# Another row order for the modulation weights, and a small read of them ahead of the conditioning vector

## The chip, the cores and the metric

The kernel runs on one core of a Trainium2 chip. The metric is the device time of one execution in microseconds (us), the median of several runs. A core has five engines with a queue of instructions each: TensorE (PE in the profile; its weight loads are PEld), VectorE (DVE), ScalarE (ACT), GpSimd (POOL) and SyncE (SP), which here only issues transfers. ScalarE issues transfers too. All transfers are carried out by the core's 16 DMA engines.

## What is computed

One transformer block whose two layer norms are modulated by a conditioning vector c. S is 2048, D is 640, all in bfloat16:

```
mod = (silu(c) @ w_mod).reshape(1, 6, 1, -1)          # w_mod: 640 x 3840
sa, ca, ga, sb, cb, gb = (mod[:, i] for i in range(6))
h = layernorm(x) * (1 + ca) + sa
x = x + ga * attention(h)      # 32 heads of 20, a causal window of 256, wqkv 640 x 1920, wo 640 x 640
h = layernorm(x) * (1 + cb) + sb
x = x + gb * mlp(h)            # (sigmoid(h @ w_gate) * (h @ w_up)) @ w_down, hidden size 1536
```

## The kernel before

The 2048 rows of x are worked on in 8 chunks of 256, each of two blocks of 128 rows. A chunk goes through layer norm 1, the transpose to hT, the projections to Q, K and V, scores and exponentials, the masks (GpSimd), the product with V, the output projection, layer norm 2 and the MLP. The chunks overlap: while one is in attention, the next ones are projected and an earlier one is in its MLP.

**The order of the work** is not found while it runs. `build` lists some 2100 operations, each with the engines it may run on, the places it reads and writes, and its working function. `PRIO` holds one number for each operation: sorted by it, they give the order on every engine, and the remainder by 5 is the engine. `schedule` gives each tile a slot of its pool, `emit` writes out each engine's queue with the semaphore waits that follow from reads, writes and reused slots. Every transfer increments one of 24 semaphores, taken in turn, and waits for the transfer 24 before it.

**The opening**, which the change touches, computes the modulation of layer norm 1 (sa and ca, that is columns 0 to 1279 of w_mod) while the first rows of x are normalised:

- ScalarE issues the transfer of c (`c_row`, 5 partitions of 128 elements), then that of the second block of x, and loads its activation table. SyncE issues the first block of x, then the five pieces of w_mod (`load_bulk`, tag wm0, one for each row group `kt`, 128 rows of 2560 bytes, kept for now in the buffer of wd), then wqkv in four pieces of 320 columns and one of 640 with further blocks of x between them, then the rest of w_mod (wm1, wm2, wm3), wo and the MLP weights. All go through the helper at L570.
- GpSimd writes the identity matrix `ident`. PE runs warm matmuls on a zeroed buffer (L649), two to an operation: three operations, then `ctr` (L634), which turns c into a column of 5 elements on each partition, then a matmul that opens the accumulators of modA, then two more warm operations.
- `ctr` is followed by VectorE's `c_col` (L636), ScalarE's tanh (L637), VectorE's `siluc` (L638) and `silubc` (L640), which spreads silu(c) over 64 columns. In VectorE's order `c_col` stands between the statistics (L776) of the first block of x and those of the second, and `silubc` ahead of those of the second.
- modA: five groups of 10 matmuls with w_mod as the weights and `silubc` as the moving side, one group for each `kt`, with filling matmuls (L660) between them. The transposes of the normalised x (with `ident` as the moving side) stand between the fourth group and the fifth. VectorE copies the result to `mA` (L761).
- The transposed x is copied to `hT` (L839) and modulated there with `mA` (L846 on ScalarE, L847 on VectorE). Then the projections of chunk 0 begin, PE reading `hT` as weights and wqkv as the moving side, and ScalarE and VectorE bring them from PSUM to `stg`, `QT`, `KT` and `V` (L893, L894).
- The first exponentials (L1015) follow on ScalarE. The transfer of the further pieces of w_mod is used later by `mod_rows` for the two gates and the modulation of layer norm 2.

c multiplies w_mod row by row, so a row of w_mod and its element of c must be on the same partition and in the same group `kt`:

```
dma(lambda: c_row, lambda: c.rearrange("o (t p) -> (o t) p", p=128), ..., eng="act")
wm_src = w_mod.rearrange("(t p) f -> p t f", p=128)
... e.matmul(psc.ap[:, 0:NDT], c_row, ident[0:NDT, 0:NDT], start=True, stop=True)
```

With these, row 128t+p is on partition p in group t.

Of the kernel before, what the change touches and what calls it, by code (L numbers as in the profile page):

```python
# [17 lines left out]
NDT = D // 128  # L18
# [7 lines left out]
SWITCH = 0.095  # L26
ENGATTR = {"pe": "tensor", "act": "scalar", "dve": "vector", "pool": "gpsimd", "sp": "sync"}
ENGS = ("pe", "act", "dve", "pool", "sp")
OVERLAP = {"pe": 0.0, "act": 0.085, "dve": 0.075, "pool": 0.045, "sp": 0.0}
# [52 lines left out]
class Prog:  # L82
# [69 lines left out]
    def schedule(self):  # L152


        free = {e: START for e in ENGS}
        bw = 0.0
        lastturn = False
        order = {e: [] for e in ENGS}
        dmacnt = [0] * NDMA
        dmalast = [None] * NDMA  # L160
        rr = 0
        pemode = 0
        portend = 0.0
        freed = {}

        def slot_time(pool, s):
            ten = pool.tenant[s]
            if ten is None:
                if not all(x.done for x in pool.init[s]):
                    return None  # L170
                return max([x.end + x.lat for x in pool.init[s]], default=0.0)
            return None if ten.left else freed[ten]

        def take(t, s):
            ten = t.pool.tenant[s]
            t.prev = list(t.pool.init[s]) if ten is None else list(ten.rel)
            t.slot = s
            t.pool.tenant[s] = t

        for o in sorted(self.ops, key=lambda x: x.prio):  # L180
            assert all(d.done for d in o.deps), o.tag
            e = ENGS[o.prio % 5]
            assert e in o.engs, (o.tag, e)
            o.eng = e
            st = max([o.tmin, free[e] + (SWITCH if e == "pe" and o.mode != pemode else 0.0)]
                     + [d.end + (0.0 if d.eng == "pe" and e == "pe" else d.lat) for d in o.deps])
            if o.isdma and e == "sp":
                st = max(st, bw - QMAX)
            for t in o.tiles:
                if t.slot is None:  # L190
                    step = 1 if t.mate is None else 2
                    best = None
                    for s in range(0, len(t.pool.tenant), step):
                        rts = [slot_time(t.pool, s + k) for k in range(step)]
                        if None not in rts and (best is None or max(rts) < best[0]):
                            best = (max(rts), s)
                    assert best is not None, (o.tag, t.name)
                    if t.mate is None:
                        take(t, best[1])
                    else:  # L200
                        take(t, best[1] + t.odd)
                        take(t.mate, best[1] + 1 - t.odd)
                for x in t.prev:
                    st = max(st, x.end + x.lat)
            if e == "dve" and o.port:
                st = max(st, free["pool"])
            elif e == "pool":
                st = max(st, portend)
            o.start = st
            if e == "pe":  # L210
                pemode = o.mout
            dur = o.dur[e]
            free[e] = st + dur - OVERLAP[e]
            if e == "dve" and o.port:
                portend = free[e]
            if o.isdma:
                turn = o.dlat > 3.0
                if e == "sp" and bw - st > 2.0:
                    free[e] += 0.35 if o.dur[e] > 1.0 else 0.1
                bw = max(st + o.dlat, bw + (MIXED if turn != lastturn and bw > st + o.dlat else 0.0)) + o.work  # L220
                lastturn = turn
                o.end = max(bw - 0.83, st + dur)
                s = rr
                rr = (rr + 1) % NDMA
                dmacnt[s] += 16
                o.key, o.val = f"d{s}", dmacnt[s]
                if dmalast[s] is not None:
                    o.deps.append(dmalast[s])
                dmalast[s] = o
            else:  # L230
                o.end = st + dur
            order[e].append(o)
            o.done = True
            for t in o.tiles:
                t.left -= 1
                if t.left == 0:
                    last = {}
                    for x in t.ops:
                        if x.isdma:
                            last[x] = x  # L240
                    for e2 in ENGS:
                        xs = [x for x in t.ops if x.eng == e2 and not x.isdma]
                        if xs:
                            last[e2] = max(xs, key=lambda x: x.start)
                    t.rel = list(last.values())
                    freed[t] = max(x.end + x.lat for x in t.rel)
        self.order = order
        self.span = max(o.end for o in self.ops)
# [88 lines left out]
def c_pe(n):  # L337
# [3 lines left out]
PE_EPS = 0.14  # L341
PRIO = [
# [124 lines left out]
START = 0.8  # L467
# [839 lines left out]
```

## Time and profile before

| | us |
|---|---|
| median of 3 runs | 325.95 |
| lowest, highest | 325.88, 325.97 |
| span of the profiled execution, first to last instruction | 324.3 |
| median less that span | 1.65 |
| PE busy | 317.3 |
| ACT busy | 212.3 |
| DVE busy | 211.8 |
| POOL busy | 187.2 |

The profile is of one execution. Its span leaves out what lies ahead of the first instruction and behind the last, 1.65 us if it took as long as the median. "Busy" is the time in which an engine has at least one instruction running; the ends of matmuls are modelled. In a timeline row stand the start, the length, the engine, the line of kernel.py, the operation, what is written and read, and in brackets the idle time ahead of it and what ended that. ACTq and SPq are the queues of ScalarE and SyncE while they issue transfers. The share of the DMA engines can pass 1, since several packets can be under way in one engine.

### The profile page before, as it was taken

The numbers are of one execution on the slowest core, as the hardware profiler recorded it, in microseconds if no ns is written. First come the engines' busy times: TensorE is split into PE (matmuls) and PEld (weight loads), VectorE is DVE, ScalarE is ACT, GpSimd is POOL, SyncE is SP. The second block draws the span as 40 slices with busy tenths as digits, with TensorE's granted clock in tenths as the row PEclk, the third lists the DMA queues.
The fourth block names the chain that finished last, engine by engine and source line by source line (L and its number), as shares of the span: only waits on it lengthen the run. The fifth ranks groups of instructions, "written<-read, shape, count | busy, mean of one in ns | idle before, by whom it ended". The sixth has DMA issues, their size and how long they took to land.

```text
span 324.3 us, 11594 instructions
## 1 busy us (share of the span) xinstructions
PE 317.3 (98%) x4872; PEld 222.7 (69%) x4873; DVE 211.8 (65%) x424; ACT 212.3 (65%) x316; POOL 187.2 (58%) x276
## 2 busy tenths in 40 slices
PE   8999999989999999999999999999999999999997
PEld 3564545446776568765776467877786788787885
DVE  5797898778687959674477475837463769264332
ACT  1899985889876687788687867786767764011120
POOL 5128869976668694847585939382939691012100
DMA  7998799989891383824405394340213032202101
GB/s 249 371 333 299 165 269 180 200 137 183 260 164 22 83 109 77 152 61 101 85 22 82 97 103 110 92 69 5 81 40 88 3 79 53 76 20 64 40 2 40
DMA packets 71694, 37.85 MB, mean 117 GB/s; under 512 B 45274, under 2 KB 70362, under 8 KB 71642
## 3 DMA queue, kind: packets, MB, share of 16 engines
q1 hardware_dynamic: 69616, 35.31, 48.3%
q10 hardware_dynamic: 2026, 1.80, 2.1%
q8 instruction: 38, 0.62, 0.8%
q14 instruction: 14, 0.11, 0.1%
HBM read 21.30 MB, written 5.25 MB: 82 GB/s over the span
## 4 chain that ended last, share of the span: by engine, by line
PE 73%; DMA 2%; SPq 2%; DVE 1%; POOL 1%; issue 0%; DVEq 0%
PE M L668 61%; PE S L669 6%; PE M L669 5%; DMA gbc<-gate 2%; SPq L803 2%; DVE wd L1192 1%; POOL x L793 0%; POOL st L788 0%; DVE hh L1211 0%; POOL E L1040 0%; DVE x L1230 0%; DVEq L310 0%
## 5 line engine op out<-in xcount | busy, mean ns | idle before, releaser
L1040 POOL TENSOR_SCALAR_AFFINE_SELECT E<-E 128x512 bf16<-128x512 bf16 (+1 forms) x176 | 142.6, 836 | 68.7 <-ACT E L1015 67.0
L1015 ACT ACTIVATE E<-S 128x512 bf16<-128x512 f32 (+2 forms) x184 | 150.9, 878 | 47.4 <-PE S L669 46.5
L668 PE MATMUL M<-wqkv,hT 128*128 128x480 bf16 (+1 forms) x340 | 73.9, 355 | 0.6 <-ACT hT L846 0.5
L668 PE MATMUL M<-h2T,wu 128*128 128x256 bf16 x480 | 68.0, 273 | 0.5 <-DVE hh L1211 0.5
L668 PE MATMUL M<-h2T,wg 128*128 128x256 bf16 x480 | 67.8, 273 | 0.0
L668 PE MATMUL M<-wd,hh 128*128 128x320 bf16 (+2 forms) x396 | 58.1, 295 | 0.0
L1209 ACT ACTIVATE sig<-M 128x512 f32<-128x512 f32 x48 | 28.9, 602 | 44.1 <-PE M L668 41.7
L1211 DVE SCALAR_TENSOR_TENSOR hh<-sig,M 128x512 bf16<-128x512 f32 x48 | 32.4, 681 | 37.1 <-ACT sig L1209 24.0
L668 PEld LDWEIGHTS M<-h2T,wu 128*128 128x128 bf16 x480 | 45.9, 98 | 8.4 <-issue 1.2
L668 PEld LDWEIGHTS M<-h2T,wg 128*128 128x128 bf16 x480 | 45.7, 98 | 7.1
L668 PEld LDWEIGHTS M<-wqkv,hT 128*128 128x128 bf16 x340 | 30.1, 98 | 27.6 <-DMA wqkv<-in_A_wqkv_dram 1.6
L668 PEld LDWEIGHTS M<-wd,hh 128*128 128x128 bf16 x396 | 36.8, 98 | 14.3 <-DVE hh L1211 0.2
L669 PEld LDWEIGHTS S<-QT,KT 20*64 20x64 bf16 (+1 forms) x1856 | 19.9, 100 | 21.3 <-ACT E L1015 12.0
L1230 DVE TENSOR_TENSOR x<-M,x 128x320 bf16<-128x320 f32 (+2 forms) x33 | 15.6, 476 | 27.2 <-PE M L668 27.2
L669 PE MATMUL S<-QT,KT 20*64 20x256 bf16 (+5 forms) x1856 | 32.1, 228 | 1.2 <-ACT E L1015 1.2
L776 DVE BATCH_NORM_STATS2 st<-x 128x6 f32<-128x320 bf16 x64 | 28.6, 477 | 2.3 <-DMA x<-in_A_x_dram 1.9
L1082 DVE STREAM_TRANSPOSE T<-M 128x512 f32<-128x512 f32 x32 | 21.5, 698 | 9.2 <-PE S L669 8.0
L668 PE MATMUL M<-wo,oT 128*128 128x320 bf16 x160 | 25.4, 299 | 0.0
L669 PE MATMUL M<-E,V 128*32 128x128 bf16 (+1 forms) x960 | 22.8, 246 | 0.8 <-ACT E L1015 0.4
L781 POOL TENSOR_SCALAR st<-st 128x2 f32<-128x2 f32 x16 | 3.7, 234 | 33.8 <-DVE st L778 33.6
L669 PEld LDWEIGHTS M<-E,V 128*32 128x32 bf16 x960 | 19.2, 97 | 5.3 <-issue 2.9
L1091 DVE STREAM_TRANSPOSE On<-Tn 128x1024 bf16<-128x1024 bf16 x16 | 19.8, 1240 | 0.3
(77 smaller groups left out, 240.2 us busy)
## 6 DMA issues: line engine op xcount, KB each, us to landing
x<-in_A_x_dram SPq DMA_DIRECT2D x23, 160.0 KB, 2.3
doc<-On SPq DMA_DIRECT2D x56, 40.0 KB
wd<-in_B_w_down_dram SPq DMA_DIRECT2D x4, 480.0 KB
wd<-in_w_mod_dram SPq DMA_DIRECT2D x5, 320.0 KB
wqkv<-in_A_wqkv_dram SPq DMA_DIRECT2D x4, 400.0 KB
wu<-in_w_mod_dram SPq DMA_DIRECT2D x5, 320.0 KB
oT<-doc SPq DMA_DIRECT2D x8, 192.0 KB, 2.5
out_dram<-x SPq DMA_DIRECT2D x9, 160.0 KB
```

What stands on the lines that cost most here:

```text
L668: return e.matmul(o, l, r, start=st, stop=sp, skip_group_check=True)
L669: return e.matmul(o, l, r, start=st, stop=sp, tile_position=tp, skip_group_check=True)
L776: A("dve", lambda e, g, bi=bi, j=j: e.bn_stats(v(bi * 12 + j * 6, 6), src[bi].ap[:, j * 320:(j + 1) * 320]), 0.48, reads=[src[bi].r()], wr ...
L781: A("pool", lambda e, g: e.tensor_scalar(v(28, n), var(), EPS, None, op0=ALU.add), 0.2, reads=[st.r(("m", bi)) for bi in range(n)], writes ...
L803: return e.dma_start_transpose(dst(), src())
L1015: A("act", lambda e, eng: e.activation(dst(), src(), ACT.Exp, scale=SM_SCALE), c_act(n), reads=[Sp.r()], writes=[E.r(key)], prio=3, tag=f" ...
L1040: A("pool", lambda e, eng: e.affine_select(rows(dst), rows(src), pattern=[[0, 8], [sign, n]], compare_op=ALU.is_ge, fill=0.0, base=base, c ...
L1082: A("dve", lambda e, g, h=h: e.transpose(T1.ap[:, 512 * h:512 * h + 512], X[h].ap), 0.694, reads=[X[h].r()], writes=[T1.r(h)], prio=3.5, t ...
L1091: A("dve", lambda e, g: e.transpose(On.ap[:], Tn.ap[:]), 1.22, reads=[Tn.r()], writes=[On.r()], prio=4, tag=f"tr2_{a}")
L1209: A("act", lambda e, g, pg=pg, sg=sg: e.activation(sg.ap[:], pg.ap[:], ACT.Tanh, scale=0.5), c_act(512), reads=[pg.r()], writes=[sg.r()], ...
L1211: A("dve", lambda e, g, pu=pu, sg=sg, f0=f0: e.scalar_tensor_tensor(out=hh.ap[:, f0:f0 + 2, :], in0=sg.ap[:].rearrange("p (a b) -> p a b", ...
L1230: A("dve", lambda e, g, ps=ps, bi=bi, c0=c0, n=n: e.tensor_tensor(x1[bi].ap[:, c0:c0 + n], ps.ap[:, 0:n], x1[bi].ap[:, c0:c0 + n], op=ALU. ...
```

## The change

- w_mod is read as `"(p t) f -> p t f"`: row 5p+t comes to partition p in group t. The number, size and order of the transfers of w_mod and of their rows in SBUF are the same.
- c is loaded in the same order, as 5 elements on each of 128 partitions (`c_pt`), and `ctr` has `ident` as its weights and `c_pt` as the moving side.
- A transfer is added, the first that ScalarE issues: columns 0 and 1 of row 5p to partition p, 4 bytes each, into a place beside `c_pt` that nothing reads. `ctr` waits for it too.
- `schedule` loses its model of times. It used the model to choose the slots; these now stand in a list, `SLOTS`, and are the ones that the model chose. `PRIO` has one entry more, for the added transfer; all other operations have the same order on every engine.

```diff
-    c_row = p_oT.aps[0][0:NDT, 0, 0:128]
+    c_pt = p_oT.aps[0][:, 0, 0:NDT]
...
-    dma(lambda: c_row, lambda: c.rearrange("o (t p) -> (o t) p", p=128), 0.05, writes=[R_crow], prio=-1, eng="act", lat=0.3)
-    wm_src = w_mod.rearrange("(t p) f -> p t f", p=128)
+    R_first = R("first")
+    dma(lambda: p_oT.aps[0][:, 0, 8:10], lambda: wm_src[:, 0, 0:2], 0.02, writes=[R_first], prio=-2, eng="act", lat=0.1, tag="first")
+    dma(lambda: c_pt, lambda: c.rearrange("o (p t) -> (o p) t", t=NDT), 0.05, writes=[R_cpt], prio=-1, eng="act", lat=0.3)
+    wm_src = w_mod.rearrange("(p t) f -> p t f", t=NDT)
...
-    p_oT.init[0].append(A("pe", lambda e, g: e.matmul(psc.ap[:, 0:NDT], c_row, ident[0:NDT, 0:NDT], start=True, stop=True), 0.1,
-      reads=[R_crow, R_ident], writes=[psc.r()], prio=0, lat=0.2, tag="ctr"))
+    p_oT.init[0].append(A("pe", lambda e, g: e.matmul(psc.ap[:, 0:NDT], ident[:], c_pt, start=True, stop=True), 0.1,
+      reads=[R_cpt, R_ident, R_first], writes=[psc.r()], prio=0, lat=0.2, tag="ctr"))
...
     for o in sorted(self.ops, key=lambda x: x.prio):
...
-                    best = None
-                    for s in range(0, len(t.pool.tenant), step):
...
+                    s = SLOTS[tiles[t]] if SLOTS else 0
```

More of the change, by code (lines that the diff above doesn't have):

```diff
@@ L25 @@
 NDMA = 24
-SWITCH = 0.095
 ENGATTR = {"pe": "tensor", "act": "scalar", "dve": "vector", "pool": "gpsimd", "sp": "sync"}
 ENGS = ("pe", "act", "dve", "pool", "sp")
-OVERLAP = {"pe": 0.0, "act": 0.085, "dve": 0.075, "pool": 0.045, "sp": 0.0}
 class Res:
@@ L152, in schedule @@
     def schedule(self):
-        free = {e: START for e in ENGS}
-        bw = 0.0
-        lastturn = False
         order = {e: [] for e in ENGS}
@@ L161, in schedule, with number @@
         rr = 0
[L162 to L178, printed above, removed]
+        tiles = {}
+        def number(t):
+            if t is not None and t not in tiles:
+                tiles[t] = len(tiles)
+                number(t.mate)
+        for o in self.ops:
+            for t in o.tiles:
+                number(t)
         for o in sorted(self.ops, key=lambda x: x.prio):
@@ L184, in schedule @@
             o.eng = e
[L185 to L188, printed above, removed]
             for t in o.tiles:
                 if t.slot is None:
-                    step = 1 if t.mate is None else 2
-                    best = None
-                    for s in range(0, len(t.pool.tenant), step):
[L194 to L215, printed above, removed]
-            if o.isdma:
[L217 to L223, printed above, removed]
-                rr = (rr + 1) % NDMA
[L225 to L231, printed above, removed]
+                    s = SLOTS[tiles[t]] if SLOTS else 0
@@ new lines, in schedule @@
+                    ten = t.pool.tenant[s]
+                    assert ten is not None or all(x.done for x in t.pool.init[s]), (o.tag, t.name)
+                    assert ten is None or ten.left == 0, (o.tag, t.name)
+                    t.prev = list(t.pool.init[s]) if ten is None else list(ten.rel)
+                    t.slot = s
+                    t.pool.tenant[s] = t
+            if o.isdma:
+                dmacnt[rr] += 16
+                o.key, o.val = f"d{rr}", dmacnt[rr]
+                if dmalast[rr] is not None:
+                    o.deps.append(dmalast[rr])
+                dmalast[rr] = o
+                rr = (rr + 1) % NDMA
@@ L237, in schedule @@
                     last = {}
[L238 to L244, printed above, removed]
+                    for x in sorted(t.ops, key=lambda x: x.prio):
+                        last[x if x.isdma else x.eng] = x
                     t.rel = list(last.values())
-                    freed[t] = max(x.end + x.lat for x in t.rel)
         self.order = order
-        self.span = max(o.end for o in self.ops)
     def emit(self):
@@ L338, in c_pe @@
     return max(n, 64) / 2400.0 + 0.0027
-PE_EPS = 0.14
 PRIO = [
[117 rows of a table removed]
[117 rows of a table added]
+]
+SLOTS = [
[20 rows of a table added]
 ]
@@ L466 @@
 DSAFE = 1.5
-START = 0.8
-PORTLAG = 0.05
-MIXED = 0.55
 NPB = 0
@@ L484 @@
 WSE = (("dve", "pool"), ("dve", "pool"))
-QMAX = 4.5
 WDT = 72.0
@@ L558, in build @@
     R_w3 = [R(f"wqkv{i}") for i in range(12)]
-    R_crow, R_ident, R_ccol, R_cth, R_siluc, R_silubc, R_wo = (R(n) for n in ("crow", "ident", "ccol", "cth", "siluc", "silubc", "wo"))
+    R_cpt, R_ident, R_ccol, R_cth, R_siluc, R_silubc, R_wo = (R(n) for n in ("cpt", "ident", "ccol", "cth", "siluc", "silubc", "wo"))
     R_wg = [[R(f"wg{t}_{h}") for t in range(NDT)] for h in range(2)]
```

254 rows, old and new, of tables (PRIO, SLOTS) are left out of this document.

## The prediction, made before the changed kernel was run

> **What bounds the kernel now.** I began with the page: the share of each engine, and the 40 slices of the span.
>
> ```profile
> span 324.3 us, 11594 instructions
> PE 317.3 (98%) x4872; PEld 222.7 (69%) x4873; DVE 211.8 (65%) x424; ACT 212.3 (65%) x316; POOL 187.2 (58%) x276
> PE   8999999989999999999999999999999999999997
> ```
>
> TensorE (PE) is busy in 317.3 of 324.3 us, and the slices show it full from the second to the last but one. The order on each engine is fixed, so an early PE start of a fraction of a microsecond is carried to the end, as long as nothing else holds it up on the way. The change touches only the opening, so the question is what makes PE begin when it does. Next came the timeline of the opening, engine by engine (start, length, engine, line, what; in brackets the idle time before it and what ended it). PE and its weight loads first:
>
> ```profile
> 1.31 2.74 PE L649 MATMUL S<-E 128*128 128x512 bf16 x6 [1.31 <-DVE E L644]
> 3.98 0.18 PE L634 MATMUL M<-ident,oT 5*128 5x5 bf16 x1
> 8.44 0.62 PE L668 MATMUL M<-ident,x 128*128 128x128 bf16 x8
> 9.01 0.45 PE L668 MATMUL S<-silubc,wd 128*128 128x64 bf16 x10
> 10.36 2.33 PE L668 MATMUL M<-wqkv,hT 128*128 128x320 bf16 x15 [0.47 <-ACT hT L846]
> ...
> 2.56 0.15 PEld L649 LDWEIGHTS S<-E 128*128 128x128 bf16 x1 [0.28 <-issue]
> 2.99 0.15 PEld L649 LDWEIGHTS S<-E 128*128 128x128 bf16 x1 [0.28 <-issue]
> 3.98 0.10 PEld L634 LDWEIGHTS M<-ident,oT 5*128 5x128 bf16 x1 [0.84 <-issue]
> 5.62 0.15 PEld L668 LDWEIGHTS S<-silubc,wd 128*128 128x128 bf16 x1 [0.28 <-issue]
> 8.10 0.35 PEld L668 LDWEIGHTS S<-silubc,wd 128*128 128x128 bf16 x10 [0.49 <-DMA wd<-in_w_mod_dram]
> ```
>
> ```profile
> 11.16 1.20 PEld L668 LDWEIGHTS M<-wqkv,hT 128*128 128x128 bf16 x10 [0.21 <-DMA wqkv<-in_A_wqkv_dram]
> 13.28 0.54 PEld L668 LDWEIGHTS M<-wqkv,hT 128*128 128x128 bf16 x5 [0.18 <-DMA wqkv<-in_A_wqkv_dram]
> 14.76 0.52 PEld L668 LDWEIGHTS M<-wqkv,hT 128*128 128x128 bf16 x5 [0.31 <-DMA wqkv<-in_A_wqkv_dram]
> ```
>
> Then VectorE (DVE) and ScalarE (ACT, with its DMA issues as ACTq), and SyncE's issues:
>
> ```profile
> 3.08 0.89 DVE L776 BATCH_NORM_STATS2 st<-x 128x6 f32<-128x320 bf16 x2 [1.42 <-DMA x<-in_A_x_dram]
> 4.20 0.17 DVE L636 TENSOR_SCALAR c_col<-M 128x5 bf16<-128x5 f32 x1 [0.23 <-PE M L634]
> 4.84 0.49 DVE L640 COPY silubc<-siluc 128x320 bf16<-128x320 bf16 x1
> 5.24 0.88 DVE L776 BATCH_NORM_STATS2 st<-x 128x6 f32<-128x320 bf16 x2
> 9.50 0.17 DVE L761 COPY mA<-S 128x10 f32<-128x10 f32 x1
> ```
>
> ```profile
> 0.79 0.57 ACTq L570 DMA_DIRECT2D oT<-in_c_dram  x1
> 1.40 0.37 ACTq L570 DMA_DIRECT2D x<-in_A_x_dram  x1
> 1.80 1.28 ACT L637 ACT_TABLE_LOAD   x1 [1.80 <-issue]
> 4.40 0.21 ACT L637 ACTIVATE cth<-c_col 128x5 f32<-128x5 bf16 x1 [1.32 <-DVE c_col L636]
> 9.77 1.65 ACT L846 ACTIVATE hT<-hT,mA 128x128 bf16<-128x128 bf16 x4
> 12.05 0.44 ACT L893 ACTIVATE stg<-M 128x320 bf16<-128x320 f32 x1 [0.29 <-PE M L668]
> 12.73 0.44 ACT L893 ACTIVATE stg<-M 128x320 bf16<-128x320 f32 x1 [0.24 <-PE M L668]
> 15.65 0.44 ACT L893 ACTIVATE stg<-M 128x320 bf16<-128x320 f32 x1 [0.21 <-PE M L668]
> 16.00 1.94 ACT L1015 ACTIVATE E<-S 128x1024 bf16<-128x1024 f32 x2
> ```
>
> ```profile
> 0.79 0.39 SPq L570 DMA_DIRECT2D x<-in_A_x_dram  x1
> 1.25 2.31 SPq L570 DMA_DIRECT2D wd<-in_w_mod_dram  x5
> ```
>
> Two chains meet at the first projection at 10.36. **The compute chain**: ctr at 3.98, c_col, tanh, silubc (4.84 to 5.33), then the statistics of the second block of x (5.24, with no idle ahead of it: VectorE was busy, x was there), the transposes of x at 8.44, the last modA at 9.01, mA at 9.50, hT at 9.77. The wait for w_mod at 8.10 delays nothing, since the transposes behind it need x. **The transfer chain**: three weight loads wait for pieces of wqkv, 0.21, 0.18 and 0.31 us, 0.70 together (a fourth, at 10.33, is over when hT is there, as the PE row at 10.36 says). SyncE issues wqkv behind the five pieces of w_mod, so wqkv lands when the stream ahead of it has passed. How fast that stream is stands in the table by stretch (stretch, its length, clock, busy share of the DMA engines, GB/s) and, for two of its stretches, in the rows of the DMA queue (packets, MB, share):
>
> ```profile
> 2.20:3.70 1.50, 1.00 0.92 279
> 3.70:5.20 1.50, 1.00 1.05 367
> 5.20:8.20 3.00, 1.00 0.98 348
> 9.00:14.00 5.00, 1.00 1.12 370
> ```
>
> ```profile
> q1 hardware_dynamic: 40, 0.10, 67.4%
> ...
> q1 hardware_dynamic: 161, 0.37, 96.6%
> ```
>
> The first of the two rows is 2.70 to 3.30, the second 6.20 to 7.20. A packet took 0.674 x 16 x 600 / 40 = 162 ns in the first and 0.966 x 16 x 1000 / 161 = 96 ns in the second. So the first packets of w_mod are slow while few bytes move. Against 370 GB/s, 2.20 to 3.70 loses 1.5 x 91/370 = 0.37 us and 5.20 to 8.20 loses 3 x 22/370 = 0.18 us: 0.55 us of stream ahead of wqkv.
>
> **The change part by part.**
>
> *ScalarE's queue.* It issues three transfers in place of two. From the starts of the rows, the first one occupies 0.79 to 1.40 and a later one 0.40 us (1.40 to 1.80). So the small read takes the place of c, c moves from 0.79 to 1.40, x1 (the second block of x) from 1.40 to 1.80, and the table load to 2.20, ending at 3.48, well ahead of the tanh. Nothing else stands in that queue.
>
> *c and the wait of ctr.* c now goes as 10 bytes to each of 128 partitions. No row shows such a transfer. By the nearest, x0 issued at 0.79 and read at 3.08, a landing takes 2.29 us: c lands at 3.69, the small read at 3.08. From below: ctr's own row says that c took at most 3.98 - 0.79 = 3.19 us. ctr also waits for the small read; behind ctr stands all of PE. The cover is the six warm matmuls: weight loads follow each other by 0.43 (2.56 to 2.99), so the sixth ends at about 3.85. c's 3.69 is 0.16 early; I take 0, and if the cover goes, each 0.1 us is 0.1 us of the compute chain. Bounds: 0 to +0.5 (a landing of 3.19 us, less the cover).
>
> *The matmul ctr.* Before, it loads 5 partitions, and its weight load comes at 3.98, not one matmul ahead as at 5.62 for a matmul at 6.04. After, it has 128x128 weights as its neighbours have, so the load can be hidden and it runs at about 3.87: -0.1 us for the compute chain. Bounds: 0 and -0.2 (its successor's load is exposed too).
>
> *x0 and x1.* x0 shares the DMA engines with the small read; its statistics end at 3.97, 0.23 ahead of c_col. x1 is issued 0.40 later but runs with a faster stream; between -0.1 and +0.4 I take 0.
>
> *The first five pieces of w_mod.* Bytes, packets and pieces stay; the row that a partition gets changes from 128t+p to 5p+t, so that each piece covers all of w_mod and a partition's five rows lie together. The small read touches that place for every partition from about 1.8, when the stream is still thin. If the slow packets are a cost of touching a region first, that cost moves ahead of the stream, and 0.55 us come back. Bounds: 0 (nothing of it was first touch) and 0.70, all that PE waits for wqkv.
>
> *Later pieces* (wm1, wm2, wm3): same bytes; in the list of PE's waits (total, times, longest) these are the only transfers that a weight load waits for, and wd there is the first five pieces:
>
> ```profile
> PEld M L668 <- DMA wqkv<-in_A_wqkv_dram: 1.6, 4, 0.9
> PEld S L668 <- DMA wd<-in_w_mod_dram: 0.7, 2, 0.5
> ```
>
> Cost 0; they are hidden by some 20 us of projections and scores. If slower reading made them late, the gates would be late first. *SLOTS and the removed planner terms*: the same tile places and order, no instruction. Cost 0.
>
> *Sum.* The third wait, at 14.76, moves to 14.21 with the stream (-0.55); the compute chain alone would allow 14.76 - 0.70 - 0.1 = 13.96, so the stream decides. ScalarE can follow: up to the exponentials at 16.00 it idles 0.29 + 0.24 + 0.21 = 0.74 us for PE. What is late next is ScalarE, then the exponentials. So 324.3 - 0.55 = 323.75 for the profiled execution. The median of 325.95 stands 1.65 above this span, and I keep that: **325.4 us**.
>
> **Two rules weighed.** The two queue rows show slow packets at 0.10 MB in 0.6 us, 170 GB/s, and quick ones at 0.37 MB in 1.0 us, 370 GB/s. The Trainium skill's "HBM Reference", section Latency, gives 0.2 us on average and 2 us at high load; by it slow packets would belong to the full stream and the small read would buy nothing, which is rival 2. The rows here go against it, since the slow ones come when the load is least.
>
> x0 and the small read are issued by different engines at the same time. The skill's "DMA: Bandwidth & Descriptors", section "Issuing engines are not separate DMA queues", says that all run on the same 16 DMA engines and interleave; by it a slow small read would hold up x0 too, which is rival 3. No run here shows the two together.
>
> **The rivals.**
> 1. *More than the sum.* Large packets need not stop at 370: 6.20 to 7.20 moved 370 at a share of 0.97, and 9 to 14 the same at 1.12. At 1.12 w_mod would move at 427, and the stream gains over 0.70; then all three waits and the 0.1 of ctr go: -0.8, 325.15.
> 2. *The change doesn't do what it says*: the slow packets are the start of any transfer, or come again at each piece. Only ctr gains, but wqkv still gates 14.76: 325.95, from -0.1 to +0.2. For it: 5.20 to 8.20 also loses. Against it: 3.70 to 5.20, between the two, is nearly full.
> 3. *The first touch comes in front of everything (slower).* The small read opens all five parts of w_mod at once; if each costs the 0.6 us stretch of 2.70 to 3.30 in turn, it lands at 3.08 + 5 x 0.6 = 6.1, ctr 2.2 late. 0.70 of that is taken up by waits that PE has anyway, so +1.5: 327.45. It turns slower by 0.2% from a ctr 1.35 us late, at 5.2. Against it: the second to fifth pieces lost only 0.18 us together.
> 4. *Rows 38,400 bytes apart read slowly (slower).* If all 640 packets took 162 in place of 96 ns, 640 x 66 / 16 = 2.6 us of stream: 328.6; half of that 327.3. Against it: wqkv, in short pieces out of every row, moved at 370.
>
> **How the numbers follow.** Forecast 0.48, rival 1 0.22, rival 2 0.10, rivals 3 and 4 0.10 each. A measurement of this kernel can tell about 0.2%, 0.65 us, from no change: below 325.3 is faster, above 326.6 slower. Half of the forecast's own range (324.95 to 325.8) and rival 1 are faster: 0.24 + 0.22 = 0.46. The other half and rival 2 are within: 0.34. Rivals 3 and 4 are slower: 0.20. The range, 324.8 to 327.4, takes in the forecast, rivals 1 and 2, and the nearer half of 3 and 4.
>
> **What would show it.** Right: 2.20 to 3.70 near 370 GB/s with packets near 100 ns; the waits for wqkv short; the load for ctr ahead of 3.98; the exponentials at 15.4 to 15.5. Wrong: ctr after 4.0, the second statistics after 5.3, wqkv still waited for at 14.7, or a shift at 16 that is not found at the end.

## The result and the profile after

| | before | after |
|---|---|---|
| median, us | 325.88 (6 runs, 325.12 to 325.97) | 326.84 (6 runs, 326.56 to 328.2) |
| ratio of the times, 95% interval | | 1.0043 [1.0029, 1.0056] |
| span of the profiled execution, us | 324.3 | 324.8 |

The changed kernel is slower, by 0.96 us of the medians; 325.4 had been forecast. The ratio goes by all the runs, of which the changed kernel has two high ones, and by it the loss is 0.9 to 1.8 us. The page of the changed kernel:

```profile
span 324.8 us, 11596 instructions
PE 317.6 (98%) x4873; PEld 223.4 (69%) x4873; DVE 212.0 (65%) x424; ACT 212.0 (65%) x316; POOL 186.4 (57%) x276
PE   7999999989999999999999999999999999999997
```

PE is as full as it was, but for the first slice, which fell from 8 to 7. So the loss lies in the opening. The timeline of PE there, and of its weight loads (the line numbers are those of the changed kernel: L602 is ctr, L636 was L668):

```profile
1.30 2.74 PE L617 MATMUL S<-E 128*128 128x512 bf16 x6 [1.30 <-DVE E L612]
5.06 0.19 PE L602 MATMUL M<-oT,ident 128*128 128x5 bf16 x1 [1.02 <-DMA oT<-in_c_dram]
5.33 1.91 PE L617 MATMUL S<-E 128*128 128x512 bf16 x4
7.04 0.74 PE L636 MATMUL S<-silubc,wd 128*128 128x64 bf16 x10
9.85 0.61 PE L636 MATMUL M<-ident,x 128*128 128x128 bf16 x8
11.77 2.28 PE L636 MATMUL M<-wqkv,hT 128*128 128x320 bf16 x15 [0.47 <-ACT hT L814]
15.56 1.25 PE L636 MATMUL M<-wqkv,hT 128*128 128x320 bf16 x8
16.75 0.40 PE L637 MATMUL S<-QT,KT 20*128 20x256 bf16 x8
```

```profile
5.06 0.10 PEld L602 LDWEIGHTS M<-oT,ident 128*128 128x128 bf16 x1 [1.92 <-DMA oT<-in_c_dram]
14.63 0.54 PEld L636 LDWEIGHTS M<-wqkv,hT 128*128 128x128 bf16 x5 [0.18 <-issue]
```

ctr, at 3.98 before, begins at 5.06. PE has done its six warm matmuls and stands idle for 1.02 us, and the bracket says for what: the transfer of c. ScalarE with its issues, and VectorE:

```profile
0.79 0.41 ACTq L536 DMA_DIRECT2D oT<-in_w_mod_dram  x1
1.23 0.45 ACTq L536 DMA_DIRECT2D oT<-in_c_dram  x1
1.71 0.45 ACTq L536 DMA_DIRECT2D x<-in_A_x_dram  x1
5.49 0.21 ACT L605 ACTIVATE cth<-c_col 128x5 f32<-128x5 bf16 x1 [2.01 <-DVE c_col L604]
11.17 1.65 ACT L814 ACTIVATE hT<-hT,mA 128x128 bf16<-128x128 bf16 x4
17.19 1.02 ACT L983 ACTIVATE E<-S 128x1024 bf16<-128x1024 f32 x1
```

```profile
3.10 0.89 DVE L744 BATCH_NORM_STATS2 st<-x 128x6 f32<-128x320 bf16 x2 [1.44 <-DMA x<-in_A_x_dram]
5.29 0.17 DVE L604 TENSOR_SCALAR c_col<-M 128x5 bf16<-128x5 f32 x1 [1.30 <-PE M L602]
6.38 0.89 DVE L744 BATCH_NORM_STATS2 st<-x 128x6 f32<-128x320 bf16 x2
```

Against the rows of before, the tanh is 5.49 - 4.40 = 1.09 us late, the modulation of hT 11.17 - 9.77 = 1.40, the first exponential 17.19 - 16.00 = 1.19. The table by stretch (start and end, length, granted clock, busy share of the DMA engines, GB/s) has no quicker stream:

```profile
2.20:3.70 1.50, 1.00 1.00 271
3.70:5.20 1.50, 1.00 0.90 291
5.20:8.20 3.00, 1.00 1.04 389
9.00:14.00 5.00, 1.00 1.12 371
```

Over the first three stretches that is (1.5 x 271 + 1.5 x 291 + 3 x 389)/6 = 335 GB/s, and before it was (1.5 x 279 + 1.5 x 367 + 3 x 348)/6 = 336. What 5.20 to 8.20 gained, 3.70 to 5.20 lost.

The spans differ by 0.5 us only, though the opening lost 1.19. Further on, PE of before and then of after:

```profile
79.25 0.82 PE L668 MATMUL M<-h2T,wu 128*128 128x256 bf16 x6
86.54 1.25 PE L668 MATMUL M<-h2T,wu 128*128 128x256 bf16 x10 [0.51 <-DVE hh L1211]
```

```profile
80.40 0.82 PE L636 MATMUL M<-h2T,wu 128*128 128x256 bf16 x6
87.01 1.25 PE L636 MATMUL M<-h2T,wu 128*128 128x256 bf16 x10
```

Near 80 us the changed kernel is still 1.15 late, from 87 on 0.47: the profiled execution of before stood idle there for 0.51, behind a gate that was spread late, and that of after didn't. The spans compare one execution with such a pause and one without; the medians (0.96) are the fairer measure. How often before has that pause isn't known; of the 14 traces of this case three show it: before (0.51), read_only (0.38) and late_ctr (0.23).

### The profile page after: what moved, and what is told of

It is laid out like the page before. It is cut to its first block, busy times and chain, and to the rows that moved or that the text cites. A ratio compares the mean times of both kernels' runs of the same rounds, so it can differ in the third digit from the quotient of the medians.

```text
span 324.8 us, 11596 instructions
## 1 busy us (share of the span) xinstructions
PE 317.6 (98%) x4873; PEld 223.4 (69%) x4873; DVE 212.0 (65%) x424; ACT 212.0 (65%) x316; POOL 186.4 (57%) x276
## 4 chain that ended last, share of the span: by engine, by line
PE 91%; ACT 3%; DVE 2%; issue 1%; DMA 1%; ACTq 0%
PE M L636 74%; PE S L637 8%; PE M L637 7%; ACT E L983 2%; DMA oT<-in_c_dram 1%; PE S L636 1%; PE S L617 1%; ACT hT L779 1%; ACTq L536 0%; DVE st L744 0%; PE S L628 0%; DVE stg L862 0%; ACT hT L807 0%; DVE Tn L1057 0%; DVE On L1059 0%
## 5 line engine op out<-in xcount | busy, mean ns | idle before, releaser
L636 PE MATMUL M<-wqkv,hT 128*128 128x480 bf16 (+1 forms) x340 | 73.7, 355 | 0.6 <-ACT hT L814 0.5
L636 PE MATMUL M<-h2T,wu 128*128 128x256 bf16 x480 | 68.1, 273 | 0.0
L636 PE MATMUL M<-h2T,wg 128*128 128x256 bf16 x480 | 67.8, 273 | 0.0
L636 PE MATMUL M<-wd,hh 128*128 128x320 bf16 (+2 forms) x396 | 58.1, 295 | 0.0
L636 PEld LDWEIGHTS M<-h2T,wu 128*128 128x128 bf16 x480 | 45.9, 98 | 7.6 <-issue 0.4
L636 PEld LDWEIGHTS M<-h2T,wg 128*128 128x128 bf16 x480 | 45.6, 98 | 7.1
L636 PEld LDWEIGHTS M<-wqkv,hT 128*128 128x128 bf16 x340 | 30.2, 98 | 27.2 <-issue 1.5
L636 PEld LDWEIGHTS M<-wd,hh 128*128 128x128 bf16 x396 | 36.8, 98 | 14.3 <-DVE hh L1179 0.2
L636 PE MATMUL M<-wo,oT 128*128 128x320 bf16 x160 | 25.4, 299 | 0.0
```

The lines of the kernel that those rows point to most:

```text
L636: return e.matmul(o, l, r, start=st, stop=sp, skip_group_check=True)
```

## The experiments

The theory after the two traces: **c is late through its place in ScalarE's queue.** At first place a transfer moves while SyncE's first block of x does; at second place it moves beside w_mod's long rows. A DMA engine takes from the two queues in turn, a packet from each, so a transfer of 128 packets (8 on each of 16 engines, if spread evenly) lasts as long as eight of w_mod's packets, and one of 5 packets hardly at all. The rivals: the small read is slow by itself, because it touches w_mod first (rival 3 of the prediction); or the 128 small packets of c, or the row order, cost the time wherever they stand. All ratios are to before, timed on the same chip. The kernels described as before with an edit, except late_ctr, place their tiles by the list `SLOTS`; in a `PRIO` list without the read's entry, 76 is c and 101 the second block of x, and 84 another operation between them.

The packets can be counted. The rows of the two queues (q1 is SyncE's, q10 ScalarE's; packets, MB, share of the engines' time) in the changed kernel from 3 to 4 us, where q10 holds c:

```profile
q1 hardware_dynamic: 122, 0.28, 92.2%
q10 hardware_dynamic: 133, 0.01, 8.2%
```

133 packets of q10 (by their size, 117 of them c's) and 122 of q1: nearly one for one, though c's take almost no time. A packet of q1 lasts 0.922 x 16 x 1000 / 122 = 121 ns, so eight turns take some 0.97 us, an estimate. By the packet records c's packets run from 2.66 to 4.50, 1.84 us, so turns of this length are about half of it; what makes up the rest isn't shown.

### no_read: the changed kernel without the small read

```diff
-    dma(lambda: p_oT.aps[0][:, 0, 8:10], lambda: wm_src[:, 0, 0:2], 0.02, writes=[R_first], prio=-2, eng="act", lat=0.1, tag="first")
-      reads=[R_cpt, R_ident, R_first], writes=[psc.r()], prio=0, lat=0.2, tag="ctr"))
+      reads=[R_cpt, R_ident], writes=[psc.r()], prio=0, lat=0.2, tag="ctr"))
```

> The changed kernel without the small read and without the wait for it; c is then ScalarE's first transfer again, issued at 0.79, still as 10 bytes to each of 128 partitions, and w_mod's rows still go out as 5p+t. Theory 1 (c's 128 small packets come behind another transfer of ScalarE's and so in turn with w_mod's first packets): c leaves ahead of w_mod, ctr runs at about 3.9 instead of 5.06, hT's first modulation at about 9.7, the time 0.2 to 0.6 us under the kernel before. Theory 2 (the small read alone holds up what is behind it): the same. Theory 3 (the row order makes w_mod's first packets slow): ctr at 3.9, but 3.70 to 5.20 stays near 290 GB/s instead of 367, and wqkv is waited for longer.

Measured: 325.26 (11 runs) against 325.66, 0.9986 [0.9976, 0.9996]. PE, VectorE and ScalarE of this kernel:

```profile
3.84 0.21 PE L601 MATMUL M<-oT,ident 128*128 128x5 bf16 x1
8.46 0.62 PE L635 MATMUL M<-ident,x 128*128 128x128 bf16 x8 [0.36 <-DVE x L763]
```

```profile
9.80 1.65 ACT L813 ACTIVATE hT<-hT,mA 128x128 bf16<-128x128 bf16 x4
15.82 1.94 ACT L982 ACTIVATE E<-S 128x1024 bf16<-128x1024 f32 x2
```

With c first, its 128 packets do no harm: they pass beside the first block of x (2.2 to 3 us: 138 packets of q1 and 144 of q10, of which 126 are c's), and ctr is 0.14 earlier than before.

```profile
q1 hardware_dynamic: 138, 0.19, 95.4%
q10 hardware_dynamic: 144, 0.00, 10.8%
```

So the whole loss comes with the small read, and the rest of the change is no loss. This kernel beats both. In the changed kernel c's last packet is 1.74 us later than here (4.50 against 2.75): c is issued 0.43 later, its first packet comes another 0.19 later, and its packets are spread over 1.84 us in place of 0.72, 1.12 more. The spreading is the largest part.

### read_only: before, with the small read ahead of c in its old form

```diff
+    dma(lambda: p_oT.aps[0][:, 1, 8:10], lambda: w_mod.rearrange("(p t) f -> p t f", t=NDT)[:, 0, 0:2], ..., eng="act", tag="first")
     dma(lambda: c_row, lambda: c.rearrange("o (t p) -> (o t) p", p=128), ..., eng="act", lat=0.3)
```

> The kernel before with the small read (row 5p, two elements for each partition) put ahead of c, and ctr waiting for both; c goes as 5 rows of 256 bytes and w_mod's rows as 128t+p, as before. Theory 1: c has five packets, one on each of five DMA engines, which get through; ctr stays at 3.98 to 4.2 and the time within 0.2 us of before. Theory 2: c is held up behind the small read, ctr at about 5, the time up by 0.5 to 1.0 us. Theory 3: as before, 3.70 to 5.20 at 367 GB/s.

Measured: 327.16 (8 runs), 1.0042 [1.0027, 1.0058]: as large a loss, by another way. Theory 1 has ctr right and the time wrong.

```profile
3.98 0.18 PE L602 MATMUL M<-ident,oT 5*128 5x5 bf16 x1
```

```profile
6.99 0.89 DVE L744 BATCH_NORM_STATS2 st<-x 128x6 f32<-128x320 bf16 x2 [1.66 <-DMA x<-in_A_x_dram]
```

ctr waits for the read here too and is on time, at 3.98 as before. So the read is not slow, and c in five packets passes at second place. What is late is the second block of x, now third: its statistics wait 1.66 us for it. Rival 3's reason falls: touching w_mod first takes no time that ctr could see. Theory 3 falls too: the stretch from 3.70 to 5.20 moved 288 GB/s with the old row order, so the 291 of the changed kernel isn't the row order's. What makes it low stays open.

### rows_only: before, with the new row order alone

```diff
-    wm_src = w_mod.rearrange("(t p) f -> p t f", p=128)
+    wm_src = w_mod.rearrange("(p t) f -> p t f", t=NDT)
```

> The kernel before with w_mod's rows as 5p+t and nothing else: c keeps its old order, so that elements of c meet other rows of w_mod than the reference's; the transfers and the work are the same in number and size. Theory 3: 2.20 to 3.70 near 270 and 3.70 to 5.20 near 290 GB/s as in the changed kernel, wqkv late by 0.3 us or more, the time up by 0.3 to 0.5 us. Theories 1 and 2: no part of the loss is in it, the time within 0.2 us of before, or below it if the row order saves slow packets.

Measured: 325.73 (12 runs), 1.0001 [0.9988, 1.0013]; 259, 380 and 377 GB/s in the three stretches. The order of the rows costs nothing that can be measured: rival 4 is out.

### c_behind_x1: no_read, with the second block of x first and c second

```diff
-    53, 58, 76, 84, 101, 99,
+    53, 58, 101, 84, 76, 99,
```

> The changed kernel without the small read, and with ScalarE's two transfers exchanged: x1 at 0.79, then c as 128 times 10 bytes at about 1.2, where the changed kernel has it. Theory 1: c's packets take turns with w_mod's first, ctr at 4.7 to 5.3, the time up by 0.4 to 1.0 us over before. Theory 2: without the small read c lands as quickly as any transfer issued at 1.2, by 3.5, and ctr runs at 3.9.

Measured: 326.73 (7 runs), 1.0023 [1.0011, 1.0036].

```profile
4.96 0.19 PE L601 MATMUL M<-oT,ident 128*128 128x5 bf16 x1 [0.92 <-DMA oT<-in_c_dram]
```

Nothing reads w_mod early here, and ctr is as late as in the changed kernel: 4.96 against 5.06. It is the second place that makes c late. Place and moment of issue go together in all these runs (first 0.79 to 0.80, second 1.23 to 1.41), so they can't be told apart; that the number of packets counts as well is shown by x1_first below.

### one_element: the changed kernel, the read cut to one partition

```diff
-    dma(lambda: p_oT.aps[0][:, 0, 8:10], lambda: wm_src[:, 0, 0:2], ...
+    dma(lambda: p_oT.aps[0][0:1, 0, 8:10], lambda: wm_src[0:1, 0, 0:2], ...
```

> The changed kernel with the small read cut to one partition (4 bytes, one packet on one DMA engine in place of 128 on 16); c and x1 stay second and third in ScalarE's queue. Place theory (whatever stands second or third there is issued 0.44 us later for each place and then takes turns with w_mod's packets): c and x1 land about as late as in the changed kernel, ctr at 4.8 to 5.1, time 0.3 to 1.0 us over before. Packet theory (the read's 128 packets hold up what is behind them): c lands early enough, ctr at 3.85 to 4.2; x1 at most 0.5 us late, time within 0.4 us of before.

Measured: 327.54 (4 runs), 1.007 [1.0053, 1.0087].

```profile
5.23 0.19 PE L602 MATMUL M<-oT,ident 128*128 128x5 bf16 x1 [1.19 <-DMA oT<-in_c_dram]
```

```profile
7.24 0.89 DVE L744 BATCH_NORM_STATS2 st<-x 128x6 f32<-128x320 bf16 x2 [0.65 <-DMA x<-in_A_x_dram]
```

One packet of 4 bytes ahead of c does as much as 128. It does more in time, 1.9 us by the medians where 0.3 to 1.0 was expected; ctr is 0.17 later than in the changed kernel, and the second block of x, third in the queue, is waited for by 0.65. What c loses is the time beside the first block of x, and any issue ahead of it takes that: c is issued at 1.35, where no_read issues it at 0.80, and by the packet records its first packet starts at 2.94, when the first block of x is over (2.76); in no_read it starts at 2.04.

### read_last: the changed kernel, the read issued third, ctr not waiting for it

```diff
-    dma(lambda: p_oT.aps[0][:, 0, 8:10], lambda: wm_src[:, 0, 0:2], 0.02, writes=[R_first], ...
+    dma(lambda: wo[:, 0, 0:2], lambda: wm_src[:, 0, 0:2], 0.02, writes=[R_first, R_wo], ...
-      reads=[R_cpt, R_ident, R_first], writes=[psc.r()], prio=0, lat=0.2, tag="ctr"))
+      reads=[R_cpt, R_ident], writes=[psc.r()], prio=0, lat=0.2, tag="ctr"))
```

The order is c, the second block of x, the read, which goes to the place of wo, loaded later.

> The changed kernel with the small read as it is, but issued by ScalarE behind c and x1, and ctr not waiting for it (its 4 bytes go into wo, which is loaded later). Place theory and packet theory: as the kernel without the read, 325.1 to 325.5, ctr at 3.84. If the read itself (touching w_mod) costs or gains something in the stream, 2.20 to 8.20 moves more or fewer bytes than without it (2.09 MB) and the time differs by 0.2 us or more.

Measured: 326.0 (10 runs), 1.0014 [1.0005, 1.0023]. ctr is at 3.84 as in no_read, and yet the kernel is slower than before, and no_read is not. Both theories were wrong on the time. The stream from 2.2 to 8.2 us moved 333 GB/s (242, 333, 378) against 348 of no_read (233, 370, 394), but before, which has no read either, moved 336, so this figure alone shows nothing. In this trace the second block of x is over at 5.14 (4.84 in no_read), its statistics wait 0.33 for it, and the first exponential is at 16.66. So the read costs something at third place too; how its 128 packets of 4 bytes do that, at under 10 ns each, stays open.

### warm_longer: the changed kernel with two more warm matmuls ahead of ctr

```diff
-        for k in range(2):
+        for n in (512, 512) + more:     # more is (512, 512) in the third operation
```

> The changed kernel with two more 512-column matmuls in the third warm operation, so that PE has work until about 4.73 and idles only to 5.06. If the gap ahead of ctr costs PE its rise to the quick rate, the first four groups of modA run in 0.45 to 0.5 us and not in 0.74, the transposes of x stand at about 9.55 in place of 9.85, and the opening is 0.2 to 0.3 us shorter. If the rise depends on time alone, nothing changes.

Measured: 327.08 (4 runs), 1.0044 [1.0029, 1.0059]. The first group of modA takes 0.50 us here, against 0.74 in the changed kernel: PE without the pause reached its quick rate sooner. What that is worth could not be read from the time, since the second block of x was later still (its statistics at 7.71, after 1.50 of waiting) and set the transposes.

### late_ctr: before, with more warm matmuls ahead of ctr

```diff
-        for k in range(2):
+        for n in (512, 512) + more:     # more is (512, 512, 256) in the third operation
```

> The kernel before with two more matmuls of 512 columns and one of 256 in the third warm operation: c and x1 land as before, only ctr comes 1.07 us late, at 5.05. If an early delay is carried to the end, the time is 0.9 to 1.2 us over before. If the gates at 78 to 86 us stand on a transfer of their own, ScalarE is about 1.1 us late at 64 us and only 0.3 to 0.6 us late behind 95 us, and the time is 0.3 to 0.6 us over before.

Measured: 326.28 (7 runs) against 325.64, 1.0022 [1.0011, 1.0033].

```profile
4.64 0.17 PE L634 MATMUL M<-ident,oT 5*128 5x5 bf16 x1
```

```profile
16.43 1.94 ACT L1015 ACTIVATE E<-S 128x1024 bf16<-128x1024 f32 x2
```

PE reached its quick rate during the added matmuls: the starts of the 512-column ones, 0.43 us apart up to 3.84, are 0.22 apart from 4.22 on. So ctr is only 0.66 late. The exponentials are 0.43 late, and the time is 0.64 longer. An early delay with no change of any transfer is carried to the end, as the prediction assumed; the interval of the time, 0.36 to 1.07 us, takes in 0.43.

### c_form_only: before, with c in its new form alone

c in 128 packets, `ident` as ctr's weights, rows of w_mod as before.

```diff
-    c_row = p_oT.aps[0][0:NDT, 0, 0:128]
+    c_pt = p_oT.aps[0][:, 0, 0:NDT]
-    ... e.matmul(psc.ap[:, 0:NDT], c_row, ident[0:NDT, 0:NDT], start=True, stop=True)
+    ... e.matmul(psc.ap[:, 0:NDT], ident[:], c_pt, start=True, stop=True)
```

> The kernel before with c as 10 bytes to each of 128 partitions, first on ScalarE's queue, and ctr with the identity matrix as its weights; no small read, and w_mod's rows stay 128t+p, so that elements of c meet other rows of w_mod than the reference's (transfers and work are the same). If the gain of the kernel without the read comes from ctr's 128x128 weights, this has all of it: ctr at 3.84, time 0.2 to 0.5 us under before. If it comes from the row order, the time is within 0.15 us of before.

Measured: 325.61 (12 runs), 0.9992 [0.9978, 1.0006]: inconclusive. ctr is at 3.84 as in no_read, but the hT modulation at 9.87 and the exponentials at 16.18 are no earlier than before. Neither the form of c nor the row order shows no_read's gain alone; whether it needs both stays open, since this interval and no_read's overlap.

### x1_first: before, with ScalarE's two transfers exchanged

```diff
-    53, 58, 76, 84, 101, 99,
+    53, 58, 101, 84, 76, 99,
```

> The kernel before with ScalarE's two transfers exchanged: x1 at 0.79, c second at 1.2, but as 5 rows of 256 bytes. Packet-turn theory (a transfer of 128 packets, eight on each DMA engine, in second place takes eight turns with w_mod's first piece, one of five packets takes one): c lands in time, ctr stays at 3.98, against 4.96 when c had 128 packets in that place; x1 lands by 3.7 in place of 5.1; the time within 0.3 us of before, or below it. Place theory alone (second place is late whatever is in it): ctr at 4.9 or later, time up by 0.4 us or more.

Measured: 325.82 (12 runs), 1.0003 [0.9991, 1.0015]. c, in five packets, goes second and ctr is at 3.98, on time. In c_behind_x1 the same place with 128 packets made it 0.98 later. The first block of x is 0.56 late (statistics at 3.64), since two blocks now take turns. In this trace that isn't hidden, since c_col stands behind these statistics on VectorE: the tanh is 0.23 late. The first group of modA took 0.74 us, the fourth waited 0.48 for w_mod, and the first exponential is 0.77 later than in before:

```profile
4.63 0.21 ACT L604 ACTIVATE cth<-c_col 128x5 f32<-128x5 bf16 x1 [1.50 <-DVE c_col L603]
16.77 1.94 ACT L982 ACTIVATE E<-S 128x1024 bf16<-128x1024 f32 x2
```

The profiled execution, 326.12, is the slowest of the twelve. The median shows nothing of it that is clear of the noise, so how much the exchange costs in time is not shown.

### c_third: before, with the second block of x first, then the read, then c in five packets

In read_only's list the read is 1:

```diff
-    53, 58, 1, 76, 84, 101, 99,
+    53, 58, 76, 101, 84, 1, 99,
```

> The kernel before with the small read, in the order x1, small read, c (5 rows of 256 bytes), ctr waiting for both. The read now stands second with 128 packets. Packet-turn theory: the read lands with w_mod's first piece, near 5, so ctr (which waits for it) runs at 4.8 to 5.2; x1 is there early; time 0.3 to 0.9 us over before. If only what stands third is late: ctr by c at 6 or later, time over 1 us above before.

Measured: 326.51 (10 runs), 1.0027 [1.0013, 1.0041]. ctr, which waits for the read and for c, is at 4.92 after 0.88 us of idle time.

```profile
4.92 0.18 PE L603 MATMUL M<-ident,oT 5*128 5x5 bf16 x1 [0.88 <-DMA oT<-in_c_dram]
```

The profile puts the end of the wait down to c, now third. By the packet records the two landed nearly together: c's last packet was over at 4.09, the read's between 4.08 and 4.22. So ctr doesn't tell which of them it waited for, but the read does: at first place, in read_only, all its packets were over by 2.83. So what delays the read is not what it reads, but where in the queue its 128 packets stand.

### wqkv_first: before, with the first piece of wqkv ahead of w_mod

```diff
-    76, 84, 101, 99, 144, 149, 154, 159, 164,
+    76, 84, 101, 99, 144, 149, 154, 159, 94,
```

> The kernel before with the first piece of wqkv issued by SyncE between x0 and w_mod's five pieces. If slow packets belong to the start of the stream, the slow stretch stays at 2.2 to 3.7 (about 280 GB/s, now wqkv) and w_mod runs at 365 and more behind it. If they belong to the first touch of w_mod, wqkv's stretch is quicker and a slow one (under 330 GB/s) follows where w_mod begins, at about 3.5 to 5. Time 0.5 to 1.5 us over before in either case, w_mod being 1.1 us later.

Measured: 325.97 (8 runs), 1.0016 [0.9998, 1.0034]. The table by stretch:

```profile
2.20:3.70 1.50, 1.00 0.74 156
3.70:5.20 1.50, 1.00 1.10 375
5.20:8.20 3.00, 1.00 1.04 411
```

Now wqkv stands in the slow stretch, at 156 GB/s, and w_mod, touched for the first time only behind it, moves at 411. wqkv's short rows alone don't explain the 156: by the packet records its packets of 640 bytes took 108 ns from 2.5 to 3 us and 33 from 3.5 on. w_mod's took 112 ns from 4.5 to 5 us, its first, where in before its first took 217 (2.5 to 3 us). The slow packets belong to the start of the stream, not to w_mod. The time was expected 0.5 to 1.5 us over before and is not clear of it.

### All transfers together

From the packet records of each trace: when the transfer was issued, when its last packet was over, and when its reader began (us). The records give queue, size and time of a packet. The read's packets have 4 bytes, like the 16 that follow each transfer of 128, so for two rows only bounds can be given.

| kernel | transfer | place, packets | issued | last packet | reader |
|---|---|---|---|---|---|
| no_read | c | first, 128 | 0.80 | 2.75 | ctr 3.84, no wait |
| read_only | c | second, 5 | 1.23 | 2.69 | ctr 3.98, no wait |
| x1_first | c | second, 5 | 1.24 | 3.28 | ctr 3.98, no wait |
| before | second block of x | second, 128 | 1.40 | 4.67 | statistics 5.24, no wait |
| after | c | second, 128 | 1.23 | 4.50 | ctr 5.06, waited |
| c_behind_x1 | c | second, 128 | 1.24 | 4.41 | ctr 4.96, waited |
| one_element | c | second, 128 | 1.35 | 4.69 | ctr 5.23, waited |
| c_third | read | second, 128 | 1.23 | 4.08 to 4.22 | ctr 4.92, waited (for c too) |
| read_only | second block of x | third, 128 | 1.85 | 6.45 | statistics 6.99, waited |
| one_element | second block of x | third, 128 | 1.75 | 6.71 | statistics 7.24, waited |
| warm_longer | second block of x | third, 128 | 1.71 | 7.22 | statistics 7.71, waited |
| after | second block of x | third, 128 | 1.71 | 5.82 | statistics 6.38, no wait |
| read_last | read | third, 128 | 1.71 | 5.84 to 6.63 | none |

128 packets take 2.0 us from their issue at first place if they have 10 bytes and 2.6 if they have 1280 (the second block of x in x1_first, over at 3.36), 2.8 to 3.3 at second place and 4.1 to 5.5 at third. The second block of x at second place took 3.3 to 3.9 in the other kernels (3.6 in no_read, 3.9 in read_last). So at second place packets of 10 and of 1280 bytes differ little; five packets need 1.5 to 2.0 there. Where the reader waited for this one transfer it began 0.49 to 0.57 us behind the last packet. In c_third ctr began 0.7 or more behind both of its transfers; why isn't shown. The Trainium skill's "DMA: Bandwidth & Descriptors", section "Queues, rings and completion order", says that each DMA engine goes round the queues for which it has work and takes a packet from each; the 122 beside 133 packets agree. The Trainium skill's section has an engine take a whole packet, typically of 9 to 17 descriptors, before it switches. What was measured differs and decides: in read_last four of the last five 4-byte packets of q10 start at 6.30, 6.40, 6.51 and 6.61, 0.105 us apart, while a row of w_mod takes 0.102, so single rows took turns.

## Why the prediction was wrong

**The failed step is "c and the wait of ctr".** It gave c a landing of 2.29 us, that of the first block of x, and so 3.69, 0.16 ahead of the end of the warm matmuls; bounds 0 to +0.5. The runs show 5.06 - 1.23 = 3.83 us from issue to ctr. A landing is no constant from the issue: the first block of x was first in its queue, and c had become second in its own. The nearest row was another, and it was in the trace of before: the second block of x was itself a transfer of 128 packets at second place. The rows of q10 in before, from 3 to 4 us, from 4 to 4.7, and the row of q1 alone that is left from 4.7 to 5.2:

```profile
q1 hardware_dynamic: 102, 0.24, 63.1%
q10 hardware_dynamic: 61, 0.08, 22.2%
...
q1 hardware_dynamic: 71, 0.16, 65.4%
q10 hardware_dynamic: 82, 0.09, 37.6%
...
q1 hardware_dynamic: 81, 0.19, 107.3%
```

It went on until 4.7, 3.3 us after its issue at 1.40. The prediction saw that its reader at 5.24 had no idle ahead of it and stopped there; these rows would have put c near 4.7 and ctr at 5 or later.

**"ScalarE's queue"** was nearly right: 0.79, 1.23, 1.71 and the table load at 2.19, where 0.79, 1.40, 1.80 and 2.20 were named. The 0.57 us of c's issue belonged to its five-row form (0.58 at second place in read_only), not to the first place. The step's consequence was missed.

**"The matmul ctr", -0.1**, was right in size: 3.98 to 3.84 in no_read and c_form_only. It didn't pass on: in no_read the transposes wait 0.36 us for x, and hT is modulated at 9.80, where it was 9.77.

**"x0 and x1".** x0 was right: 3.10 against 3.08. x1 was taken at 0 within -0.1 and +0.4; in the changed kernel its last packet is 5.82 - 4.67 = 1.15 later than in before. That is hidden there only because silubc is late itself, and in read_only, where it is not, x1 alone costs the whole loss.

**"The first five pieces of w_mod", -0.55**, failed twice. The first touch was wrong: wqkv_first shows the slow start with another tensor, and from 2.2 to 8.2 us the stream was no faster with the read (335 GB/s in the changed kernel) than without it (336 in before, 348 in no_read). Rival 2's reason, that slow packets are the start of any transfer, was the right one. And the price was too high. The three waits of 0.70 us are idle time of the weight loads, which is not PE's. From the first projection to the first scores the lag of after behind before falls from 11.77 - 10.36 = 1.41 to 15.56 - 14.21 = 1.35 and to 16.75 - 15.55 = 1.20: with no wait for wqkv left, 0.21 us came back. The wait of 0.18 us is even still there, at 14.63, under the name of issue. At most 0.21 of the forecast 0.55 could have come.

**Rival 3** had the direction and the place (ctr late, all of PE behind it), with a wrong reason. It took 0.70 us of lateness as taken up by waits and put its turning point at 1.35; only 0.21 was, so 1.08 of lateness was enough.

**How 1.09 became 1.40 and then 1.19.** Between the tanh and hT another 0.31 us was lost. In the changed kernel the first two groups of modA take 0.74 us where before they take 0.58 and then 0.46, and the filling matmuls beside them are slower too (0.61 and 0.38 us); the quick rate comes only after 9 us. In the four kernels where PE stood idle for 0.88 us or more ahead of ctr (after, c_behind_x1, one_element, c_third) it comes between 8.9 and 10 us, in those without between 4.2 and 7.1. That the pause causes this is the likely reading, but not shown: without a pause too the moment varies by some 3 us. warm_longer, made to price it, could not, for x1. The Trainium skill's "TensorE: Matmul & The Clock Gate" section "What's actually happening", states that the quick rate needs some 3.4 us of sustained work and that the moment varies from run to run. The rows agree in size: about 4.1 us from ctr at 5.06 in the changed kernel, 4.9 and 3.2 from the first warm matmul in before and in no_read, and from 2.9 (late_ctr) to 5.8 (x1_first) in the kernels without a pause. Then 0.21 came back at the waits for wqkv: 1.09 + 0.31 - 0.21 = 1.19.

**That an early shift is carried to the end** was right: late_ctr, and 1.15 still at 80 us. All the traces agree. Their first exponentials start between 15.82 (no_read) and 18.26 (warm_longer), 2.4 us apart, and yet from there to the end of the span it is 307.6 to 307.8 us in ten of the 14. The other four have 308.0 to 308.3: the three with the pause near 87, and read_last.

## What to carry to other kernels

When a transfer is put into a queue, count the packets per DMA engine of everything behind it, and ask which transfer of the other queue each will now take turns with; price it by a row of the same place and number of packets, not by the nearest landing. A small transfer that must go behind another wants few packets, not few bytes. And idle time listed for the weight loads is time of PE only as far as the next matmul starts late: compare the starts of the matmuls before it is counted as a gain.

## What was not expected of the hardware

- 128 packets of 10 bytes, 1.3 KB in all, needed 3.0 to 3.3 us from issue to the last packet at second place of the queue and 2.0 at the first; as many bytes in five packets needed 1.5 to 2.0 at second place.
- The start of the stream is slow whichever tensor stands there: 156 to 351 GB/s from 2.2 to 3.7 us in the kernels here, the least where the first piece was wqkv, with rows of 640 bytes. Its cause stays open.
- The same ten matmuls take 0.74 us early and 0.46 later at a granted clock of 1.00 throughout: the column doesn't show this change of rate, the durations of equal groups do.
